# Sketched attention and a gated convolution on one core: tokens of a chunk in the order (m, j), stores by group

## The chip, the cores and the metric

The kernel runs on one core of a Trainium2 chip. The metric is the device time of one execution in microseconds (us), the median over the runs of the unchanged kernel.

## What is computed

The inputs are q, k and v of shape 4 x 4 x 1088 x 32 (batch, heads, tokens, head dimension), two sketch matrices S1 and S2 of 8 x 32, and three weights. Attention is linear: both q and k become 64 features, products of two sketches of 8. Its output, heads side by side, is x of 4 x 1088 x 128; xp is x with K - 1 = 4 rows of zeros ahead of each batch, so the gate is a causal convolution of 5 taps for each channel.

```python
def phi(x):
    a = np.einsum('rd,bhsd->bhsr', S1, x)
    b = np.einsum('rd,bhsd->bhsr', S2, x)
    return np.einsum('bhsi,bhsj->bhsij', a, b).reshape(*x.shape[:-1], r * r)
q_p, k_p = (phi(q), phi(k))
kv = np.einsum('bhsf,bhsd->bhfd', k_p, v)
z = np.sum(k_p, axis=2)
num = np.einsum('bhsf,bhfd->bhsd', q_p, kv)
den = np.einsum('bhsf,bhf->bhs', q_p, z)[..., None] + 1e-06
return (num / den).astype(np.float32)
...
x = np.ascontiguousarray(attn_out.transpose(0, 2, 1, 3)).reshape(B, S, H * D)
...
for k in range(K):
    gate_pre += conv_w[k][None, None, :] * xp[:, k:k + S, :]
gate = 1.0 / (1.0 + np.exp(-gate_pre))
val = x @ w_val
return (gate * val @ w_out).astype(np.float32)
```

## The kernel before

The 1088 tokens of a batch are seen as 32 values of m times 34 values of t, token = 34 m + t, so that one m is a contiguous piece of 34 tokens in memory. The t are cut into two units, U = 0 with t from 16 to 33 and U = 1 with t from 0 to 15, and into four groups of 8 or 10 t (`GROUPS`). The last two t (32 and 33) are the leftover, `v_lo` and `osb_lo`. For products with tokens on the partitions a chunk of 128 tokens is 4 values of j times 32 values of m, with t = 8 j + c for k and v and t = t0 + 4 j + c at the output.

All work is cut into steps with names of four characters: two letters for the kind, a digit for the batch (0 to 3) and a digit for a unit, group or part. The table `ORDER` lists all steps, and the loop at the end of the kernel issues them in that order, so it sets the order of instructions on each engine; numbers behind a colon are the PSUM banks (`ring`) that a step uses. Nothing is rescheduled. Each engine works off its own instructions in order.

The kinds are, in the order in which a batch passes through them: `ld` loads (0 and 1 the weights, from ACT's queue; 2 and 3 the halves of k with t below 16 and from 16 on, 4 and 5 those of q from 16 on and below 16, 6 v in four transfers, one for a head, 7 the leftover of v in two; all from SP's queue). `kt` transposes k on DVE, `kp` multiplies it with the sketches on PE, `ke` copies the result to SBUF on ACT (`kab`), `ko` forms the 64 features (`phik`) on POOL or DVE, `kv` sums them against v and z on PE. `pv`, `pz`, `pm`, `pe` turn these sums into weights (`wq`, `kvb`). `qt`, `qp`, `qc`, `qd`, `qo` do the same for q, with the denominator (`phi`), `qx` transposes on PE, `qe` copies (`phiT`), `nm` multiplies with kv, `xe` copies to `xe`, and `hl` shifts the first columns. `gt` is the convolution and `vl` the value product on PE, `sg` the sigmoid on ACT, `gv` their product on DVE, `om` the output product on PE, `oe` its copy to `osb` on ACT, and `so` the stores from SP's queue. `cn` are constants, `cn06` nine matmuls on zeros ahead of the real ones, `cn05` the casts of two weights on POOL. The sets `KO_DVE` and `QO_POOL` say which products go to DVE and which to POOL.

Every load has a buffer of its own, for each batch, so no load waits for compute.

Of the kernel before, what the change touches and what calls it, by code (L numbers as in the profile page):

```python
# [24 lines left out]


ORDER = """
cn08 ld00 cn00 ld02 cn06:01 ld03 cn07 ld06 cn09 ld01 ld07 cn02
cn01 ld05 kt00 ld04 ld13 ld12 kt01 ld15 kp00:2 ld16 kp01:3 ke00
ko00 ko03 ke01 ko02 ko08 ko09 ld23 cn03:4 ko06 cn04 cn05 ld17  # L30
ko05 ko01 ko07 kv00 qt01 ld14 ld22 kv01 ld26 qt00 pv00 pz00
pm00:5 kt11 pe00 ld25 qp00:6 kt10 ld32 ld33 qp01:0 qc00 ld35 qt11
kp10:1 ld24 qc01 qd00 kp11:3 ld27 ke10 ko12 ke11 ld36 ko13 qd01
ko11 qo01 ko16 ld37 ko10 qo00 qx01:2 ko18 kv10 qo02 qe01 ld34
ko17 qx00:4 qt10 qx02:5 ko15 nm01:1 qe00 qo03 qe02 ko19 nm00:3 kt21
qx03:6 xe01 nm02:2 kv11 xe00 hl00 kt20 qe03 xe02 nm03:4 pz10 pv10
kp20:0 xe03 pm10:5 qt21 ke20 kp21:1 pe10 ko20 ko21 gt01:36 ke21 ko23
kt30 vl03:2 vl02:4 sg03 ko25 ko27 qp10:5 sg02 gv03 ko22 gv02 qp11:0
qc10 kt31 ko29 om01:6 kv20 qc11 qd10 ko28 oe01 kp30:1 ko26 so01
kp31:3 qt20 ke30 qo10 kv21 qo11 gt00:24 ko31 pv20 ko32 ke31 pz20  # L40
ko33 vl01:6 qd11 sg00 pm20:5 sg01 ko39 qx11:1 pe20 vl00:2 qx10:4 qe11
ko30 gv01 qp20:5 qe10 qo13 ko36 nm11:1 kv30 qc20 qo12 ko37 xe11
nm10:6 gv00 ko38 qx13:4 ko35 qx12:1 xe10 om00:02 qd20 qe13 hl10 kv31
qe12 oe00 nm13:3 nm12:6 pz30 qp21:4 qo21 qo20 pv30 so00 xe12 xe13
pm30:1 qt30 qc21 qx20:0 gt11:26 pe30 qd21 qe20 vl12:5 vl13:3 sg13 nm20:1
qx21:0 sg12 gv13 qp30:6 xe20 qo23 gv12 qe21 qt31 om11:4 gt10:23 qc30
qo22 oe11 qd30 vl10:1 so11 vl11:5 sg10 nm21:0 sg11 qx23:4 qp31:2 xe21
gv11 qe23 hl20 qx22:3 gv10 qc31 nm23:0 qo31 qe22 qo30 om10:54 xe23
nm22:1 qd31 oe10 qx30:3 gt20:60 xe22 so10 qe30 vl20:4 vl21:5 qo33 qo32
qx31:1 sg20 nm30:3 sg21 gv20 qx33:6 qe31 gt21:20 gv21 qe33 vl23:4 vl22:1  # L50
xe30 nm31:5 nm33:6 sg23 qx32:3 xe31 gv23 qe32 om20:05 hl30 xe33 nm32:4
oe20 gt30:36 xe32 so20 vl30:0 sg22 vl31:5 sg30 gt31:42 gv22 sg31 gv30
om21:3 gv31 sg33 vl32:1 vl33:6 sg32 om30:02 oe21 gv33 gv32 oe30 so21
om31:5 so30 oe31 so31
""".split()


# [1 line left out]
def kernel(  # L59
# [94 lines left out]
    def s_const(b, i):  # L154
        if i == 0:
            nc.gpsimd.memset(mask1, 1.0)
            for sgn, base in ((1, 0), (-1, 31)):
# [10 lines left out]
        elif i == 9:
            make_identity(nc, ident32)
            make_identity(nc, ident)  # L170
            for t in range(2):
                nc.gpsimd.memset(pden[t], 1e-6)
                nc.gpsimd.memset(xe[t][:, 0:4, 0:1], 0.0)
                nc.gpsimd.memset(kvb[t], 0.0)
        elif i == 1:
            nc.vector.transpose(sT[:, 0, :], s1raw)
            nc.vector.transpose(sT[:, 1, :], s2raw)
            for t in range(2):
                nc.vector.tensor_mul(
                    wq[t][:, 0:64].rearrange("p (k h r) -> p k h r", k=2, h=H),  # L180
                    bc(sT[:, :, 0:r], 2, [P, 2, H, r]),
                    bc(bc(mask1, 1, [P, 2, 4]), 3, [P, 2, 4, r]),
                )
        elif i == 2:
            nc.vector.tensor_reduce(
                out=mask2, in_=mask16.rearrange("p c h -> p h c"), axis=AX.X, op=ALU.add
            )
            nc.vector.tensor_mul(
                s2rep.rearrange("p (h d) -> p h d", h=H),
                bc(s2raw, 1, [P, H, D]),  # L190
                bc(mask2, 2, [P, H, D]),
            )
        elif i == 3:
            nc.tensor.transpose(bank("cn", b, i)[:, 0:Kconv], cw_in, ident32[:Kconv, :Kconv])
        elif i == 4:
            nc.scalar.copy(out=cwT, in_=bank("cn", 0, 3)[:, 0:Kconv])
# [4 lines left out]
        elif i == 5:
            nc.gpsimd.tensor_copy(out=wv, in_=wv_f)
            nc.gpsimd.tensor_copy(out=wo, in_=wo_f)
# [8 lines left out]
    def s_ld(b, i):
# [9 lines left out]
        elif i in (2, 3, 4, 5):  # L222
            x, y = ((k, k_in), (q, q_in))[i // 4]
            t0, n = ((0, 16), (16, 18), (16, 18), (0, 16))[i - 2]
            nc.sync.dma_start(  # L225
                out=y[b][:, t0 * D : (t0 + n) * D],
                in_=x[b].rearrange("h (m t) d -> (h m) (t d)", m=M)[:, t0 * D : (t0 + n) * D],
            )
        elif i == 6:
            for h in range(H):  # L230
                nc.sync.dma_start(  # L231
                    out=v_in[b][:, h, :],
                    in_=v[b, h].rearrange("(m t) d -> m (t d)", m=M)[:, 0:1024].rearrange("m (j x) -> j m x", j=4),
                )
        elif i == 7:
            for j in range(2):
                nc.sync.dma_start(
                    out=v_lo[b][j * 32 : j * 32 + 32],
                    in_=v[b].rearrange("h (m t) d -> m h t d", m=M)[:, :, 32 + j, :],
                )  # L240

    def s_kt(b, u):
        o = kT[b % 2][:, 0:32, :].rearrange("p (c j) m -> p j c m", j=4)[:, 2 * u : 2 * u + 2]
        i_ = k_in[b][:, 0 : 32 * D].rearrange("p (j c d) -> p j c d", j=4, c=8)[:, 2 * u : 2 * u + 2]
        nc.vector.transpose(o, i_)  # L245
# [14 lines left out]
    def s_ke(b, u):  # L260
        nc.scalar.copy(out=kab[u][:, :, 0 : 4 + u, :], in_=kab_view(b, u))  # L261
# [153 lines left out]
    def s_gv(b, g):  # L415
# [4 lines left out]
        nc.vector.tensor_mul(  # L420
            o[:, 0:512].rearrange("p (c j m) -> p j c m", c=4, j=4)[:, 2 * w : 2 * w + 2], view(gate[g]), view(vl)
        )
        if g == 1:
            nc.vector.tensor_mul(o[:, 512:576], gate[g][:, 256:320], vl[:, 256:320])

    def s_om(b, U):
# [10 lines left out]
        if U == 0:  # L437
            nc.scalar.copy(out=osb_lo[b], in_=bank("om", b, U, 1)[0:64, 0:P])

    def s_so(b, U):  # L440
        t0, n = UNITS[U]
        dst = out[b].rearrange("(m t) e -> m t e", m=M)
        nc.sync.dma_start(
            out=dst[:, t0 : t0 + 16, :].rearrange("m (j c) e -> j m (c e)", j=4),
            in_=osb[2 * b + U].rearrange("p c e -> p (c e)"),
        )
        if U == 0:
            nc.sync.dma_start(out=dst[:, 32:34, :].rearrange("m j e -> j m e"), in_=osb_lo[b])
# [39 lines left out]
```

## Time and profile before

| | us |
|---|---|
| median of 3 runs | 75.9 (75.12 to 76.77) |
| the profiled execution | 74.68 |
| its span, from the first to the last instruction | 72.8 |

Busy time over the span is 48.5 on PE, 38.6 on DVE, 35.1 on ACT and 27.2 on POOL. The span is the part that the trace shows; 1.88 us of the profiled execution lie around it. In the rows of the prediction a stretch of the span, 35.00:59.83 for instance, is followed by its length and by the busy time of each engine in it with the number of instructions in brackets. A line such as L245 is a line of the listing above. A row of waits names who waited, for whom, the total in us, how many times and the longest. SPq is SP's sequencer, which issues the transfers, and its durations are those of an issue, not of a transfer.

### The profile page before, as it was taken

How to read it: one execution, taken by the hardware profiler on the slowest of the kernel's cores; microseconds unless marked ns; L12 is line 12 of the kernel's file. 1: busy time of each engine (PE TensorE's matmuls, PEld its weight loads, DVE VectorE, ACT ScalarE, POOL GpSimd, SP SyncE). 2: the span in 40 equal slices, each digit the busy share in tenths (PEclk: the TensorE clock that was granted, in tenths of full speed). 3: DMA queues.
4: the chain of work that ended last, by engine and by line, in shares of the span. 5: the costliest groups of instructions: out<-in, count | busy, mean ns of one | idle time of the engine just before them, and what ended most of it. 6: DMA issues, size and time to landing. Idle time of an engine off the chain costs nothing.

```text
span 72.8 us, 2687 instructions
## 1 busy us (share of the span) xinstructions
PE 48.5 (67%) x1114; PEld 37.3 (51%) x1114; DVE 38.6 (53%) x103; ACT 35.1 (48%) x100; POOL 27.2 (37%) x58
## 2 busy tenths in 40 slices
PE   3962949689537599946999999999998950000000
PEld 1312927479426379824978887877786630000000
DVE  1029477666991931079998979969852540000000
ACT  0800490121523746722449799989999891000000
POOL 5900345000499500991199816655731000000000
PEclk9999655555999857999999999999999999655555
DMA  0935469838753499532563201222222222222220
GB/s 0 285 118 155 128 217 279 300 105 222 242 166 108 139 304 297 170 111 91 131 197 106 101 35 18 62 81 36 82 74 88 62 52 96 48 99 101 98 94 11
DMA packets 7645, 9.30 MB, mean 128 GB/s; under 512 B 1869, under 2 KB 4562, under 8 KB 7634
## 3 DMA queue, kind: packets, MB, share of 16 engines
q1 hardware_dynamic: 6888, 8.91, 39.5%
q10 hardware_dynamic: 746, 0.23, 1.5%
q8 instruction: 8, 0.13, 0.7%
q14 instruction: 3, 0.02, 0.1%
HBM read 6.92 MB, written 2.23 MB: 126 GB/s over the span
## 4 chain that ended last, share of the span: by engine, by line
DMA 32%; PE 27%; SPq 9%; ACT 7%; DVE 4%; issue 3%; DVEq 0%; ACTq 0%
PE ring L138 18%; DMA k_in<-in_k_dram 12%; DMA q_in<-in_q_dram 11%; DMA v_in<-in_v_dram 9%; SPq L231 6%; PE kv L138 5%; PE ring L375 4%; SPq L225 3%; ACT phiT L381 2%; ACT gate L409 2%; ACT osb L436 2%; DVE gv L420 1%; DVE kT L245 1%; DVE qT L323 1%; PE ring L309 1%
## 5 line engine op out<-in xcount | busy, mean ns | idle before, releaser
L268 POOL TENSOR_TENSOR phik<-kab 128x256 f32<-128x256 f32 x26 | 15.4, 626 | 15.8 <-ACT kab L261 15.5
L381 ACT COPY phiT<-ring 128x512 bf16<-128x512 bf16 (+1 forms) x16 | 9.4, 617 | 3.6 <-PE ring L375 2.9
L361 POOL TENSOR_TENSOR phi<-an,bc_sb 128x512 bf16<-128x512 f32 (+1 forms) x6 | 7.3, 1217 | 6.9 <-DVE an L353 3.5
L138 PE MATMUL ring<-wq,qT 128*64 128x96 f32 x144 | 8.7, 278 | 1.4 <-DVE phik L268 1.1
L323 DVE STREAM_TRANSPOSE qT<-q_in 128x512 f32<-128x512 f32 (+1 forms) x8 | 5.9, 742 | 6.2 <-DMA q_in<-in_q_dram 6.1
L138 PE MATMUL kv<-phik,v_in 128*32 128x64 f32 x256 | 7.8, 256 | 1.9 <-DMA v_in<-in_v_dram 1.1
L138 PEld LDWEIGHTS ring<-wq,qT 128*64 128x64 f32 x144 | 7.6, 159 | 1.9 <-DVE phik L268 1.3
L375 PE MATMUL ring<-ident,phi 128*64 128x128 bf16 (+1 forms) x144 | 7.0, 224 | 2.2 <-DVE phi L361 2.2
L420 DVE TENSOR_TENSOR gv<-gate,ring 128x256 bf16<-128x256 bf16 x16 | 6.2, 415 | 3.3 <-ACT gate L409 3.2
L138 PE MATMUL ring<-wq,kT 128*64 128x64 f32 x144 | 6.3, 242 | 1.9 <-DVE kT L245 1.9
L138 PEld LDWEIGHTS kv<-phik,v_in 128*32 128x32 f32 x256 | 5.8, 129 | 3.3 <-DMA v_in<-in_v_dram 1.3
L361 DVE TENSOR_TENSOR phi<-an,ring 128x512 bf16<-128x512 f32 (+1 forms) x10 | 7.0, 728 | 0.3 <-POOL phik L268 0.2
L375 PEld LDWEIGHTS <-phi 128*64 128x64 bf16 (+1 forms) x144 | 5.4, 112 | 3.4 <-DVE phi L361 2.5
L138 PEld LDWEIGHTS ring<-wq,kT 128*64 128x64 f32 x144 | 5.8, 155 | 2.7 <-DVE kT L245 2.5
L138 PE MATMUL ring<-xe,diag 64*64 64x256 bf16 (+1 forms) x160 | 6.5, 280 | 0.0
L261 ACT COPY kab<-ring 128x256 f32<-128x256 f32 (+1 forms) x8 | 3.2, 399 | 6.6 <-PE ring L138 6.1
L391 ACT CAST xe<-ring 128x256 bf16<-128x256 f32 (+1 forms) x16 | 6.2, 400 | 0.4 <-PE ring L138 0.4
L409 ACT ACTIVATE gate<-ring 128x256 bf16<-128x256 f32 (+1 forms) x16 | 5.6, 405 | 0.5 <-PE ring L138 0.5
L245 DVE STREAM_TRANSPOSE kT<-k_in 128x512 f32<-128x512 f32 x8 | 5.5, 692 | 0.6 <-DMA k_in<-in_k_dram 0.6
L342 ACT COPY bc_sb<-ring 128x320 f32<-128x320 f32 (+3 forms) x8 | 2.8, 355 | 5.2 <-PE ring L138 5.1
L138 PE MATMUL ring<-phiT,kvb 128*64 128x256 bf16 (+1 forms) x32 | 4.7, 306 | 0.7 <-ACT phiT L381 0.6
L436 ACT COPY osb<-ring 128x512 f32<-128x512 f32 x8 | 4.7, 602 | 0.9 <-PE ring L138 0.8
(56 smaller groups left out, 66.1 us busy)
## 6 DMA issues: line engine op xcount, KB each, us to landing
v_in<-in_v_dram SPq DMA_DIRECT2D x16, 128.0 KB
out_dram<-osb SPq DMA_DIRECT2D x8, 256.0 KB
k_in<-in_k_dram SPq DMA_DIRECT2D x4, 288.0 KB
q_in<-in_q_dram SPq DMA_DIRECT2D x4, 288.0 KB
k_in<-in_k_dram SPq DMA_DIRECT2D x4, 256.0 KB
q_in<-in_q_dram SPq DMA_DIRECT2D x4, 256.0 KB
v_lo<-in_v_dram SPq DMA_DIRECT2D x8, 16.0 KB
out_dram<-osb_lo SPq DMA_DIRECT2D x4, 32.0 KB
```

Of the source, the lines that this page charges most:

```text
L138: nc.tensor.matmul(o, lhsT=lhsT, rhs=rhs, start=start, stop=stop, skip_group_check=True, **kw)
L231: nc.sync.dma_start(out=v_in[b][:, h, :], in_=v[b, h].rearrange("(m t) d -> m (t d)", m=M)[:, 0:1024].rearrange("m (j x) -> j m x", j=4),)
L245: nc.vector.transpose(o, i_)
L268: (nc.vector if dve else nc.gpsimd).tensor_mul(phik[u][:, c].rearrange("p h (i j) -> p h i j", i=r), bc(a_, 3, [P, H, r, r]), bc(b_, 2, [P ...
L323: nc.vector.transpose(flat(qT[b % 2][:, t0 : t0 + n, :]), q_in[b][:, t0 * D : (t0 + n) * D])
L361: (nc.gpsimd if pool else nc.vector).tensor_mul(phi[(4 * b + g) % 3][:, 0:n, :].rearrange("p c (i j) -> p c i j", i=r), bc(an[U][:, lo : l ...
L375: nc.tensor.transpose(o[64 * (h % 2) : 64 * (h % 2) + 64, h // 2, c * P : c * P + n], phi[(4 * b + g) % 3][:n, 4 * c + h, :], ident[:n, :n],)
L381: nc.scalar.copy(out=phiT[(4 * b + g) % 3][:, :, 0 : GROUPS[g][1] * M], in_=pt_view(b, g))
L391: nc.scalar.copy(out=flat(xe[b % 2][:, 4 + t0 : 4 + t0 + n, :]), in_=bank("nm", b, g)[:, 0 : n * M])
L409: nc.scalar.activation(out=gate[g][:, 0:n], in_=bank("gt", b, g // 2, g % 2)[:, 0:n], func=ACT.Sigmoid)
L420: nc.vector.tensor_mul(o[:, 0:512].rearrange("p (c j m) -> p j c m", c=4, j=4)[:, 2 * w : 2 * w + 2], view(gate[g]), view(vl))
L436: nc.scalar.copy(out=osb[2 * b + U].rearrange("p c e -> p (c e)"), in_=bank("om", b, U))
```

## The change

A chunk of 128 tokens now has its tokens in the order (m, j) instead of (j, m). So the transfers of v and the stores have m, with 32 values, as outermost dimension where they had j, with 4 or 2. Four things follow from it: the transposed k (`kT`) is written with j as the innermost dimension, so neighbours are 4 elements apart; `gv` is written in the same way, 2 elements apart; a chunk's two halves of 64 partitions belong to one group each, so each group is stored by itself (two stores of 64 partitions for a unit in place of one of 128); and the matmul of `kp` takes 64 adjoining columns. Apart from that, the second `wq` is copied from the first, the tables `KO_DVE` and `QO_POOL` are other, with one phi product less on POOL, and `ORDER` is a new table.

```diff
-cn08 ld00 cn00 ld02 cn06:01 ld03 cn07 ld06 cn09 ld01 ld07 cn02
+cn08 ld00 cn09 ld04 cn06:01 ld03 cn07 ld02 ld05 ld07 cn00 ld01
...
-    kT = [st(f"kT{i}", [P, NT, M]) for i in range(2)]
+    kT = [st(f"kT{i}", [P, NT * M]) for i in range(2)]
...
-            for t in range(2):
-                nc.vector.tensor_mul(
-                    wq[t][:, 0:64].rearrange("p (k h r) -> p k h r", k=2, h=H),
...
+            nc.vector.tensor_mul(
+                wq[0][:, 0:64].rearrange("p (k h r) -> p k h r", k=2, h=H),
...
         elif i == 2:
+            nc.vector.tensor_copy(out=wq[1][:, 0:64], in_=wq[0][:, 0:64])
...
-                    in_=v[b, h].rearrange("(m t) d -> m (t d)", m=M)[:, 0:1024].rearrange("m (j x) -> j m x", j=4),
+                    in_=v[b, h].rearrange("(m t) d -> m (t d)", m=M)[:, 0:1024].rearrange("m (j x) -> m j x", j=4),
...
-        o = kT[b % 2][:, 0:32, :].rearrange("p (c j) m -> p j c m", j=4)[:, 2 * u : 2 * u + 2]
+        o = kT[b % 2][:, 0:1024].rearrange("p (c m j) -> p j c m", c=8, m=M)[:, 2 * u : 2 * u + 2]
...
-            t = 16 * u + 4 * c
-            two = [t, t + 2] if c < 4 else [32, 32]
+            t = 512 * u + P * c
             for z in range(2):
-                mm(o[64 * z : 64 * z + 64, :, c, :], flat(kT[b % 2][:, two[z] : two[z] + 2, :]), wq[0][:, 0:64])
+                lt = kT[b % 2][:, t + 64 * z : t + 64 * z + 64] if c < 4 else kT[b % 2][:, 1024:1088]
+                mm(o[64 * z : 64 * z + 64, :, c, :], lt, wq[0][:, 0:64])
...
-            o[:, 0:512].rearrange("p (c j m) -> p j c m", c=4, j=4)[:, 2 * w : 2 * w + 2], view(gate[g]), view(vl)
+            o[:, 0:512].rearrange("p (c w m j) -> p w j c m", c=4, w=2, m=M)[:, w], view(gate[g]), view(vl)
...
-    def s_so(b, U):
-        t0, n = UNITS[U]
+    def s_so(b, g):
+        t0, n = GROUPS[g]
+        w = g % 2
         dst = out[b].rearrange("(m t) e -> m t e", m=M)
         nc.sync.dma_start(
-            out=dst[:, t0 : t0 + 16, :].rearrange("m (j c) e -> j m (c e)", j=4),
-            in_=osb[2 * b + U].rearrange("p c e -> p (c e)"),
-        )
-        if U == 0:
-            nc.sync.dma_start(out=dst[:, 32:34, :].rearrange("m j e -> j m e"), in_=osb_lo[b])
...
+            out=dst[:, t0 : t0 + 8, :].rearrange("m (j c) e -> m j (c e)", j=2),
+            in_=osb[2 * b + g // 2][64 * w : 64 * w + 64].rearrange("p c e -> p (c e)"),
+        )
+        if g == 1:
+            nc.sync.dma_start(out=dst[:, 32:34, :], in_=osb_lo[b])
```

Below, a number behind a name is that of a buffer: q_in_75 to q_in_78, k_in_71 to k_in_74, v_in_79 to v_in_82 and v_lo_83 to v_lo_86 belong to batches 0 to 3, osb_125 to osb_132 to unit 0 and 1 of batches 0 to 3 in turn, phik_93 and kab_91 to the chunks with u = 0 and phik_94 and kab_92 to those with u = 1.

The start of SP's queue, the loads of batch 0 and the first of batch 1:

```order
+L225 DMA q_in_75<-in_q_dram 128x576
+L225 DMA k_in_71<-in_k_dram 128x576
 L225 DMA k_in_71<-in_k_dram 128x512
-L225 DMA k_in_71<-in_k_dram 128x576
+L225 DMA q_in_75<-in_q_dram 128x512
+L237 DMA v_lo_83<-in_v_dram 32x4x32 x2
 L231 DMA v_in_79<-in_v_dram 128x1x256 x4
-L237 DMA v_lo_83<-in_v_dram 32x4x32 x2
-L225 DMA q_in_75<-in_q_dram 128x512
-L225 DMA q_in_75<-in_q_dram 128x576
+L225 DMA k_in_72<-in_k_dram 128x512
 L225 DMA k_in_72<-in_k_dram 128x576
```

Both halves of q now stand ahead of v, and one of them ahead of k. Up to q of batch 2 (the last part of q_in_77) the new queue has q and k of three batches, v of two, and the leftovers of three, 26 transfers; v of batch 2, which stood ahead of it, stands behind k of batch 3.

PE between the weights of batch 0 (`pm00`) and the first transposes of phi, before:

```order
L138 MATMUL ring_69<-zm_95,s2rep 64x32 x2
L309 MATMUL ring_69<-ident_139,kvf_97 128x128
L138 MATMUL ring_70<-wq_101,qT_89 64x3x32 x10
L138 MATMUL ring_64<-wq_101,qT_89 64x3x32 x8
L138 MATMUL ring_65<-wq_101,kT_88 64x2x32 x8
L138 MATMUL ring_67<-wq_101,kT_88 64x2x32 x10
```

and now:

```order
L138 MATMUL ring_69<-zm_95,s2rep 64x32 x2
L309 MATMUL ring_69<-ident_139,kvf_97 128x128
L138 MATMUL ring_70<-wq_101,kT_88 64x2x32 x8
L138 MATMUL ring_64<-wq_101,qT_89 64x3x32 x10
L138 MATMUL ring_65<-wq_101,kT_88 64x2x32 x10
L138 MATMUL ring_66<-wq_101,qT_89 64x3x32 x8
```

The two halves of `kp` of batch 1 (kT_88) moved ahead of one half of `qp` of batch 0 (qT_89) each. On POOL the two weight casts (`cn05`) moved from behind the first two products of batch 0 to ahead of them, and of batch 1's nine products `ko` two went to DVE.

The end of SP's queue, the stores of batch 2 and 3, before:

```order
L443 DMA out_dram<-osb_129 4x32x512
L448 DMA out_dram<-osb_lo_135 2x32x128
L443 DMA out_dram<-osb_130 4x32x512
L443 DMA out_dram<-osb_131 4x32x512
L448 DMA out_dram<-osb_lo_136 2x32x128
L443 DMA out_dram<-osb_132 4x32x512
```

and now:

```order
L445 DMA out_dram<-osb_130 32x2x512 x2
L445 DMA out_dram<-osb_129 32x2x512 x2
L450 DMA out_dram<-osb_lo_135 32x2x128
L445 DMA out_dram<-osb_131 32x2x512 x2
L450 DMA out_dram<-osb_lo_136 32x2x128
L445 DMA out_dram<-osb_132 32x2x512 x2
```

Each store of 4 x 32 pieces became two of 32 x 2, and behind the copy of the last unit (osb_132) two stores follow in place of one.

More of the change, by code (lines that the diff above doesn't have):

```diff
@@ L36 @@
[L36 to L51, printed above, removed]
@@ L55 @@
+qo33 qe30 vl23:5 so10 qo32 vl22:1 sg23 qx33:3 nm30:0 sg22 nm31:2 gv23
+xe30 qx32:6 gv22 xe31 gt20:45 qe33 hl30 qe32 om21:0 nm33:2 sg20 vl20:1
+vl21:3 nm32:6 xe33 gv20 sg21 gt30:42 xe32 gv21 oe21 vl31:1 sg31 om20:56
+so23 vl30:3 sg30 gt31:02 gv31 so22 oe20 gv30 vl32:4 vl33:1 sg33 so20
+om30:56 sg32 gv33 so21 oe30 gv32 om31:3 so30 oe31 so31 so32 so33
 """.split()
@@ L246, in s_kt @@
         if u == 1:
-            nc.vector.transpose(flat(kT[b % 2][:, 32:34, :]), k_in[b][:, 32 * D : 34 * D])
+            nc.vector.transpose(kT[b % 2][:, 1024:1088], k_in[b][:, 32 * D : 34 * D])
     def kab_view(b, u):
```

42 lines of the change are left out of this document (27 added, 15 removed).

## The prediction

> **What bounds the kernel now.** I read the page's slices first, then the chain that ended last, then the busy time by stretches that I cut where the slices change.
>
> ```profile
> span 72.8 us, 2687 instructions
> PE   3962949689537599946999999999998950000000
> PEclk9999655555999857999999999999999999655555
> DMA  0935469838753499532563201222222222222220
> HBM read 6.92 MB, written 2.23 MB: 126 GB/s over the span
> DMA 32%; PE 27%; SPq 9%; ACT 7%; DVE 4%; issue 3%; DVEq 0%; ACTq 0%
> ...
> 3.67 6.73 DMA v_in<-in_v_dram
> ...
> 14.07 8.55 DMA k_in<-in_k_dram
> ...
> 23.22 8.13 DMA q_in<-in_q_dram
> ...
> 59.86 0.58 ACT osb L436
> ```
>
> There are three parts. Until 31.35 (23.22 + 8.13) the chain is made of loads and their issue. Then compute runs to 60.44 (59.86 + 0.58), with PE at nine tenths. Then come 12.4 us (72.8 - 60.44) with all engines still and only the DMA row at 2 tenths.
>
> ```profile
> 6.48:20.00 13.52, 10.45 (x204) 8.79 (x204) 9.21 (x24) 4.55 (x16) 3.32 (x7) 0.62 0.69 210
> 20.00:35.00 15.00, 10.66 (x283) 8.39 (x283) 8.36 (x19) 6.83 (x19) 8.86 (x16) 0.89 0.55 172
> 35.00:59.83 24.83, 23.78 (x626) 18.91 (x618) 18.99 (x54) 21.64 (x63) 12.21 (x16) 1.00 0.28 80
> 64.00:71.00 7.00, 0.00 (x0) 0.00 (x0) 0.00 (x0) 0.00 (x0) 0.00 (x0) 0.50 0.26 98
> 71.00:72.80 1.80, 0.00 (x0) 0.00 (x0) 0.00 (x0) 0.00 (x0) 0.00 (x0) 0.50 0.03 11
> ...
> 25.00:30.00 5.00, 5.00 (x123) 4.08 (x121) 1.34 (x4) 2.55 (x9) 1.02 (x3) 0.68 0.97 283
> ...
> SPq L483 <- DMA out_dram<-osb: 9.2, 1, 9.2
> ...
> SPq L237 <- DMA v_in<-in_v_dram: 5.0, 3, 2.3
> ...
> POOL phik L268 <- ACT kab L261: 15.5, 3, 7.0
> DVE qT L323 <- DMA q_in<-in_q_dram: 6.1, 3, 3.8
> ```
>
> Columns are the stretch and its length, then PE, PEld, DVE, ACT and POOL busy time, granted clock, DMA share, GB/s. In 64 to 71 only stores are left: share 0.26 and 98 GB/s, about 4 of 16 engines at 25 GB/s each. With all engines busy (25 to 30) the same hardware moves 283 GB/s at 0.97. Every transfer whose outermost dimension is 4 (v_in, osb) is confined to a quarter of the engines, and whatever is spread over all of them (k_in, q_in) waits for that quarter. That is why POOL, DVE and PE starve before 35.
>
> **The change, part by part.**
>
> *1. The tail.* The rows at the end:
>
> ```profile
> 59.85 0.54 SPq L443 DMA_DIRECT2D out_dram<-osb  x1
> 60.48 0.62 SPq L448 DMA_DIRECT2D out_dram<-osb_lo  x1
> 61.20 1.29 SPq L443 DMA_DIRECT2D out_dram<-osb  x1
> ...
> L443 SPq DMA_DIRECT2D out_dram<-osb x8: 537/548/1288, 35.4 to 61.2; - x8
> ...
> L231 SPq DMA_DIRECT2D v_in<-in_v_dram x16: 531/532/755, 1.7 to 32.7; - x16
> ...
> 59.53 0.28 ACT L438 COPY osb_lo<-ring 64x128 f32<-64x128 f32 x1
> ...
> 0.80 0.88 SPq L225 DMA_DIRECT2D k_in<-in_k_dram  x2
> ...
> 1.50:2.00 0.50, 0.50 (x2) 0.15 (x1) 0.00 (x0) 0.00 (x0) 0.38 (x3) 1.00 0.36 66
> ```
>
> After, the last stores are two for unit 0, one small, two for unit 1. At 0.55 each (median 0.548) five take 2.75, and four gaps of 0.09 (59.85 + 0.54 to 60.48) make 3.1. They begin when the copy of unit 0 is done, about 0.9 before that of unit 1 ends (0.58 for it and 0.28 for osb_lo between), so SP is through 2.2 after the last copy. Before it was 2.05 (61.20 + 1.29 - 60.44), so the doubled issues cost next to nothing: the long last issue, which waited for the queue, pays for them. Then the first byte: the first load, issued at 0.80 for 0.44, shows 33 KB in the stretch 1.5 to 2.0, so bytes from about 1.88, 0.65 after its issue. The last 131 KB at 283 GB/s take 0.47. From the last bytes (20 KB move after 71.0, so to about 71.1) to the end of the span are 1.7. Sum: 2.2 + 0.65 + 0.47 + 1.7 = 5.0 instead of 12.4, a gain of 7.4. Ends: 4.4 if one issue less is left behind the copy, 6 if the last two stores follow one another at half the rate.
>
> [...]
>
> *2. Loads.* The 2.1 MB of v now use all engines, so the whole stream goes at 283 GB/s. What DVE waited for until 31.37, q of batch 2, has 4.5 MB of k, q and v up to its own end in the new SP order (front part), plus 0.2 MB of weights: 4.7 / 0.283 = 16.6, from 1.9 on, plus 1.7 to its semaphore as at the span's end: 20. k of batch 3, 0.56 MB more, lands by about 22. SP's issue is not in the way: 26 transfers up to there at 0.53, the median of v's (k and q take less), are 13.8. From 20 on no engine should wait for loads. What is late next is compute.
>
> *3. The first 20 us.* Here latency, not bandwidth, sets the pace.
>
> ```profile
> 4.90 0.29 DVE L188 TENSOR_TENSOR s2rep<-s2raw,mask 128x128 f32<-128x128 f32 x1 [2.64 <-DMA s2raw<-in_S_dram]
> ...
> 5.72 1.29 DVE L245 STREAM_TRANSPOSE kT<-k_in 128x512 f32<-128x512 f32 x2
> ...
> 6.48 0.33 PE L138 MATMUL ring<-wq,kT 128*64 128x64 f32 x2 [1.60 <-DVE kT L245]
> ...
> 15.01 3.14 PE L138 MATMUL ring<-wq,qT 128*64 128x96 f32 x36 [0.28 <-ACT wq L313]
> 17.94 1.25 PE L138 MATMUL ring<-wq,kT 128*64 128x64 f32 x36
> ...
> 11.12 0.40 POOL L203 CAST wo<-wo_f 128x256 bf16<-128x256 f32 x1 [1.01 <-DMA wo_f<-in_moe_w_out_dram]
> ...
> 19.15 5.29 POOL L268 TENSOR_TENSOR phik<-kab 128x256 f32<-128x256 f32 x9 [7.05 <-ACT kab L261]
> ...
> L323 DVE STREAM_TRANSPOSE qT<-q_in 128x512 f32<-128x512 f32 x4 | 2.8, 710 | 4.6 <-DMA q_in<-in_q_dram 4.5
> ```
>
> One q transpose (at least 0.71, as the smaller half has it) and the constants now stand ahead of the first kT on DVE, so the first kp starts about 1.0 later, near 7.5. The v wait that follows (v landed at 10.4) goes, since v of batch 0 is 1.7 MB into the stream (landing near 9.5). Both casts stand ahead of all products on POOL, and the cast of wo waited until 11.12 for its load. POOL's products take 0.59 (5.29 / 9). Of batch 0's three only the last stood behind that cast: 11.5 + 0.6 = 12.1. If the load comes no earlier, the three now end near 13.3; if it lands at 10, near 12.2. I take the first qp at 15.3, and PE at 20.0 where it was. What is gained is order: the first half of kp of batch 1 now runs ahead of qp, POOL has seven products of batch 1 instead of nine (two went to DVE, which idles there), and the last five start behind the second half of kp, near 18.2: 18.2 + 5 x 0.59 = 21.1, three us sooner than 24.4 (19.15 + 5.29). kv of batch 1 follows them.
>
> *4. From 20 on.* PE's rate when nothing starves it is 23.78 / 626 = 0.038 per matmul. The 283 + 626 = 909 left at 20.0 need 34.5, so PE could end at 54.5 and ended at 59.83: 4.3 were lost before 35 (15.0 - 283 x 0.038) and 1.05 after. Of the 4.3 I give back 3.0: loads and POOL, which caused the waits, come early, but the chain phi, phiT, nm, xe of batch 0 leaves PE thin near 20, and a stretch at clock 0.5 may come again (the mean in 20 to 35 is 0.89). Ends: 0 and 4.3. ACT needs 6.83 + 21.64 = 28.5 after 20 and DVE 27.4, both below PE.
>
> *5. Strides.*
>
> ```profile
> L245 DVE STREAM_TRANSPOSE kT<-k_in 128x512 f32<-128x512 f32 x8 | 5.5, 692 | 0.6 <-DMA k_in<-in_k_dram 0.6
> L420 DVE TENSOR_TENSOR gv<-gate,ring 128x256 bf16<-128x256 bf16 x16 | 6.2, 415 | 3.3 <-ACT gate L409 3.2
> ```
>
> kT is now written with 16 bytes between neighbours, gv with 4. kT already is scattered by blocks and costs 692 against 710 for the plain qT of the same size, so I take 0; the other end is twice the time, 5.5 + 6.2 = 11.7 on DVE. A gain is left out, as qT, written in one piece, is no faster. One phi product goes from POOL to DVE and one product for wq becomes a copy, less than 1 us of DVE together; its idle time (15.0 - 8.36 before 35) hides that, and under the second rival it would not.
>
> **Sum.** Compute ends at 60.44 - 3.0 = 57.4; with 5.0 the span is 62.4 instead of 72.8, minus 10.4. The profiled execution took 74.68 (1.88 outside its span), 1.2 below the median 75.9: 64.3 by the one, 65.5 by the other. I say 64.9, midway, that is 2.5 above the span, here and for the rivals.
>
> **Rivals.**
> - *Only the tail goes.* ACT is busy 21.64 of 24.83 in the dense stage and the later start of kp is real; then compute ends at 60.4 and the time is 60.4 + 5.0 + 2.5 = 67.9.
> - *The strides cost.* With 11.7 more, DVE needs 36.4 after 20 (27.4, half of kT's 5.5 and all of gv's 6.2), more than PE's 34.5: with 2 to 3 of waits compute ends near 59, and the time is 66.5. Against it speaks the kT row above. [...]
> - *PE runs dense from 20 on.* The 4.3 go whole, and the last 1.05 too: compute ends at 55.1, the time is 62.6.
> - *It does not do what it says.* If 4 engines stay, the tail and the loads stay: 75 to 76. The 0.97 with k_in and q_in (outermost 128) speaks against it.
> - *Slower.* If the split follows the dimension that counts j wherever it stands, it is 2 for the stores now. Then 2.23 MB go at 2 x 25 = 50 GB/s, 44.6 us. In the new order no output matmul stands ahead of kv of batch 3, and some 16 us of PE work stand behind the first, so the first store comes near 40: span 86, time 89. It turns into a loss when the stores get less than about 65 GB/s (2.23 MB in 33 us). The rows can't tell the place of the 4 from its being 4.
>
> [...]
>
> **How the numbers follow.** Both gains 0.60, tail alone 0.18, strides 0.08, dense 0.08, no effect 0.03, slower 0.03. Changes over 2% are about what a measurement of this kernel can tell from none. Faster by over 2% holds the first four, 0.94; within 2% 0.03; slower 0.03. The range reaches from the dense case with a tail of 4.4 (61.5) to the tail alone with a tail of 6 (69).
>
> **What would show it.** Right: after the last osb copy under 6 us, a DMA share above 0.5 while stores run, no DVE wait of over 1 us for q_in, the last PE instruction between 55 and 58.5, kT still near 0.69. Wrong: share 0.26 or 0.13 at the end; kT near 1.4; PE at clock 0.5 beyond 22; PE gaps between 20 and 30 released by ACT or DVE rather than DMA, which would make the order the bound.

## The result, and the profile after

| | before | changed |
|---|---|---|
| median, us | 76.34 (75.12 to 77.3, 4 runs) | 65.1 (64.98 to 65.72, 4 runs) |
| the profiled execution | 74.68 | 64.98 |
| its span | 72.8 | 63.0 |
| the last copy to osb ends | 60.44 | 56.80 |
| from there to the end of the span | 12.4 | 6.2 |

The ratio is 0.864, with a 95% interval of 0.852 to 0.876. The forecast was 64.9. Of the 9.8 us that the span lost, 6.2 went from the tail and 3.6 from compute. Some executions are disturbed and a little longer; ratios leave them out, and medians here are over all runs of a kernel.

The page of the changed kernel, its slices (a slice is now 1.575 us) and its chain:

```profile
span 63.0 us, 2682 instructions
PE   2990019388799959997999999999979998920000
DVE  1015991991935999999999999995898916730000
ACT  0630002650421407788248999599999999970000
PEclk9999855555555899999999999999999999999655
DMA  0799469988669993773400000019136530386650
PE 30%; DVE 27%; ACT 22%; DMA 6%; issue 2%; ACTq 1%; DVEq 1%
```

The chain was a third DMA; now it is compute, and of the DMA share only one load is left, that of S2 at the very start. DMA is busy until slice 20 and then only while stores run, where before it dragged on at 1 and 2 tenths from slice 25 to the end. The 2 tenths of the tail have become 5 and 6, and the tail is short.

Busy time by stretches of the changed kernel (columns as in the prediction):

```profile
6.48:20.00 13.52, 9.13 (x180) 8.02 (x182) 9.02 (x19) 3.87 (x14) 3.73 (x7) 0.53 0.79 241
20.00:35.00 15.00, 13.80 (x431) 11.41 (x427) 14.57 (x35) 8.73 (x25) 11.30 (x19) 0.96 0.52 160
...
20.00:30.00 10.00, 8.80 (x241) 7.13 (x237) 9.78 (x21) 5.91 (x17) 6.44 (x12) 0.95 0.71 213
30.00:40.00 10.00, 10.00 (x355) 8.54 (x357) 9.62 (x26) 7.02 (x22) 7.95 (x13) 1.00 0.09 30
40.00:56.80 16.80, 14.82 (x341) 11.30 (x339) 11.82 (x34) 16.25 (x46) 4.75 (x6) 1.00 0.42 97
```

Up to 20 PE is behind where it was (180 matmuls, before 204). Then it is far ahead: 431 against 283 in 20 to 35. The bound wanders: DVE is full from 20 to 30 (9.78 of 10), PE from 30 to 40 (10.00), ACT from 40 to the end (16.25 of 16.80). No engine waits for k_in, q_in or v_in any more.

The start, rows of the timeline on DVE, PE and POOL:

```profile
5.31 0.21 DVE L177 STREAM_TRANSPOSE sT<-s2raw 128x32 f32<-128x32 f32 x1 [0.66 <-DMA s2raw<-in_S_dram]
...
6.42 0.77 DVE L323 STREAM_TRANSPOSE qT<-q_in 128x576 f32<-128x576 f32 x1
7.11 1.04 DVE L245 STREAM_TRANSPOSE kT<-k_in 128x512 f32<-128x512 f32 x1
...
8.12 1.02 DVE L245 STREAM_TRANSPOSE kT<-k_in 128x512 f32<-128x512 f32 x1
...
9.20 2.19 PE L138 MATMUL ring<-wq,kT 128*64 128x64 f32 x36 [4.49 <-DVE kT L245]
...
17.83 1.81 PE L138 MATMUL ring<-wq,qT 128*64 128x96 f32 x20
...
7.86 0.40 POOL L203 CAST wo<-wo_f 128x256 bf16<-128x256 f32 x1 [0.77 <-DMA wo_f<-in_moe_w_out_dram]
...
21.32 2.97 POOL L268 TENSOR_TENSOR phik<-kab 128x256 f32<-128x256 f32 x5 [1.51 <-ACT kab L261]
```

and the groups of the two tiles that are written at a stride (group rows of the page):

```profile
L245 DVE STREAM_TRANSPOSE kT<-k_in 128x512 f32<-128x512 f32 x8 | 8.5, 1090 | 0.0
...
L420 DVE TENSOR_TENSOR gv<-gate,ring 128x256 bf16<-128x256 bf16 x16 | 6.6, 439 | 2.8 <-ACT gate L409 2.4
```

The k transpose takes 1090 ns where it took 692. The first kp waits for two of them and starts at 9.20, where it was 6.48 before and 7.5 in the forecast. Before, two matmuls of kp could start when one half of kT was written, and the other 34 stood at 7.07:

```profile
7.07 1.63 PE L138 MATMUL ring<-wq,kT 128*64 128x64 f32 x34 [0.26 <-DVE kT L245]
```

Now 64 adjoining columns hold all four values of j, so even the first matmul needs both halves. The cast of wo, on the other hand, is over at 8.26, long before POOL's first product needs the engine.

The end, rows of the timeline on ACT and SP and stretches of the tail:

```profile
56.21 0.59 ACT L437 COPY osb<-ring 128x512 f32<-128x512 f32 x1 [0.33 <-PE ring L138]
...
53.32 2.46 SPq L445 DMA_DIRECT2D out_dram<-osb  x4
55.87 0.55 SPq L450 DMA_DIRECT2D out_dram<-osb_lo  x1
56.51 1.19 SPq L445 DMA_DIRECT2D out_dram<-osb  x2
57.79 0.55 SPq L450 DMA_DIRECT2D out_dram<-osb_lo  x1
58.44 1.19 SPq L445 DMA_DIRECT2D out_dram<-osb  x2
...
59.63:60.20 0.57, 0.00 (x0) 0.00 (x0) 0.00 (x0) 0.00 (x0) 0.00 (x0) 0.50 0.93 212
60.20:60.70 0.50, 0.00 (x0) 0.00 (x0) 0.00 (x0) 0.00 (x0) 0.00 (x0) 0.50 0.88 205
60.70:61.20 0.50, 0.00 (x0) 0.00 (x0) 0.00 (x0) 0.00 (x0) 0.00 (x0) 0.50 0.34 78
```

From 53.32 on SP issues without a pause, ten stores in 6.3 us, so the last one is issued 2.8 behind the last copy (59.63). From there on some 260 KB move, both of the last stores (0.57 x 212 + 0.50 x 205 + 0.50 x 78), at 205 to 212 GB/s with the engines at 0.9.

### The profile page after: what moved, and what is told of

It reads as the page before. It is cut to its first block, busy times and chain, and to the rows that moved or that the text cites. A ratio compares the mean times of both kernels' runs of the same rounds, so it can differ in the third digit from the quotient of the medians.

```text
span 63.0 us, 2682 instructions
## 1 busy us (share of the span) xinstructions
PE 46.2 (73%) x1114; PEld 36.1 (57%) x1114; DVE 41.7 (66%) x104; ACT 34.5 (55%) x100; POOL 25.6 (41%) x57
## 4 chain that ended last, share of the span: by engine, by line
PE 30%; DVE 27%; ACT 22%; DMA 6%; issue 2%; ACTq 1%; DVEq 1%
PE ring L138 19%; DVE kT L245 11%; PE kv L138 9%; ACT phiT L381 7%; DMA s2raw<-in_S_dram 6%; ACT gate L409 5%; ACT osb L437 5%; DVE phi L361 4%; ACT xe L391 3%; PE ring L375 2%; DVE phik L268 2%; DVE qT L323 2%; DVE den L351 2%; DVE pden L350 1%; ACT bc_sb L342 1%
## 5 line engine op out<-in xcount | busy, mean ns | idle before, releaser
L138 PE MATMUL ring<-wq,kT 128*64 128x64 f32 x144 | 7.2, 271 | 5.1 <-DVE kT L245 4.5
L261 ACT COPY kab<-ring 128x320 f32<-128x320 f32 (+1 forms) x8 | 3.2, 399 | 10.4 <-PE ring L138 9.6
L245 DVE STREAM_TRANSPOSE kT<-k_in 128x512 f32<-128x512 f32 x8 | 8.5, 1090 | 0.0
L361 DVE TENSOR_TENSOR phi<-an,ring 128x512 bf16<-128x512 f32 (+1 forms) x11 | 7.9, 748 | 0.1
L361 POOL TENSOR_TENSOR phi<-an,bc_sb 128x512 bf16<-128x512 f32 (+1 forms) x5 | 5.7, 1158 | 4.4 <-DVE zm L297 2.6
L138 PE MATMUL kv<-phik,v_in 128*32 128x64 f32 x256 | 6.6, 245 | 1.2 <-POOL phik L268 1.0
L138 PEld LDWEIGHTS kv<-phik,v_in 128*32 128x32 f32 x256 | 5.0, 124 | 2.2 <-POOL phik L268 1.2
L323 DVE STREAM_TRANSPOSE qT<-q_in 128x576 f32<-128x576 f32 (+1 forms) x8 | 5.8, 724 | 0.0
L268 DVE TENSOR_TENSOR phik<-ring,kab 128x256 f32<-128x256 f32 x10 | 3.7, 414 | 2.4 <-ACT kab L261 2.4
L138 PEld LDWEIGHTS <-diag 64*64 64x64 bf16 x160 | 4.4, 106 | 1.3 <-issue 0.8
```

The costliest lines, as they stand in the source:

```text
L138: nc.tensor.matmul(o, lhsT=lhsT, rhs=rhs, start=start, stop=stop, skip_group_check=True, **kw)
L268: (nc.vector if dve else nc.gpsimd).tensor_mul(phik[u][:, c].rearrange("p h (i j) -> p h i j", i=r), bc(a_, 3, [P, H, r, r]), bc(b_, 2, [P ...
L323: nc.vector.transpose(flat(qT[b % 2][:, t0 : t0 + n, :]), q_in[b][:, t0 * D : (t0 + n) * D])
L361: (nc.gpsimd if pool else nc.vector).tensor_mul(phi[(4 * b + g) % 3][:, 0:n, :].rearrange("p c (i j) -> p c i j", i=r), bc(an[U][:, lo : l ...
```

## Experiments

Twelve kernels were measured in three groups of four; those of a group ran on the same chip. "First kp" is the start of the first matmuls of kp on PE, "compute ends" the end of the last copy to osb, both from the profiled execution.

### The loads alone, the stores alone, both, under the old order table

Both the loads of v and the stores can have 32 outermost values without a new token order, if a transfer takes one j instead of one head or one unit: then m is outermost, and the tokens stay in the order (j, m). For v this needs as many transfers as before, for the stores four times as many. Three kernels do one, the other, and both, with everything else as in the kernel before.

```diff
-            for h in range(H):
+            for j in range(4):
                 nc.sync.dma_start(
-                    out=v_in[b][:, h, :],
-                    in_=v[b, h].rearrange("(m t) d -> m (t d)", m=M)[:, 0:1024].rearrange("m (j x) -> j m x", j=4),
+                    out=v_in[b][32 * j : 32 * j + 32, :, :],
+                    in_=v[b].rearrange("h (m t) d -> m h (t d)", m=M)[:, :, 256 * j : 256 * j + 256],
                 )
...
-        nc.sync.dma_start(
-            out=dst[:, t0 : t0 + 16, :].rearrange("m (j c) e -> j m (c e)", j=4),
-            in_=osb[2 * b + U].rearrange("p c e -> p (c e)"),
-        )
+        for j in range(4):
+            nc.sync.dma_start(
+                out=dst[:, t0 + 4 * j : t0 + 4 * j + 4, :].rearrange("m c e -> m (c e)"),
+                in_=osb[2 * b + U][32 * j : 32 * j + 32].rearrange("p c e -> p (c e)"),
+            )
         if U == 0:
-            nc.sync.dma_start(out=dst[:, 32:34, :].rearrange("m j e -> j m e"), in_=osb_lo[b])
+            for j in range(2):
+                nc.sync.dma_start(out=dst[:, 32 + j, :], in_=osb_lo[b][32 * j : 32 * j + 32])
```

Loads alone:

> The kernel before, only v's loads cut by j instead of by head, so that m with 32 values is their outermost dimension; token order, stores and order table as before. Theory of the prediction (confined loads starve compute until 35): the last copy to osb ends near 57 instead of 60.4, no wait of DVE for q_in over 1 us, but the tail stays at 11 to 12.5, since the stores stay on 4 engines: 71.5 to 73. Rival (the new order table is what makes compute end earlier): compute ends at 60 still, 75 to 76.

Stores alone:

> The kernel before, only the stores cut by j, four of 32 partitions for a unit with m as outermost dimension, and two for the leftover; loads and order table as before. Theory: compute ends at 60.4 as before, and the tail is bound by SP's issue, some 10 stores at 0.6 behind the copy of unit 0 and then 3.4 to the end: 8.9 behind the last copy instead of 12.4, so 71 to 73. Rival (tail bound by the engines' rate, whatever the issues): 5 to 6, so 68 to 69.

Both:

> Both at once, with the order table of before. Theory: the gains add, compute ends near 57 and the tail is 8.9: 67.5 to 69.5. Rival (the order table is needed for the gain of compute): 71 to 73, as with the stores alone.

| | median, us | ratio to before (95%) |
|---|---|---|
| loads alone | 72.97 (71.98 to 73.85) | 0.940 (0.929 to 0.950) |
| stores alone | 71.77 (70.64 to 73.56) | 0.926 (0.909 to 0.943) |
| both | 68.21 (67.44 to 69.05) | 0.888 (0.875 to 0.901) |

All three times lie where the theory had them, and none where a rival had it. By ratios the gains are 6.0% and 7.4%, together 11.2%, so most of the sum is kept. The loads end compute earlier and the stores shorten the tail. With the loads alone (a profile of 73.85) the last copy ends at 58.54, not quite the 57 expected, and the tail is 13.4; DVE's waits for q_in, 6.1 before, are gone. With the stores alone (a profile of 71.91) it ends at 62.37 and the tail is 7.8, and those waits are there still:

```profile
DVE qT L323 <- DMA q_in<-in_q_dram: 5.7, 3, 3.9
```

The kernel with both has both gains in its profile (PE's first kp, ACT's last copy, SP's last issues):

```profile
6.80 0.33 PE L138 MATMUL ring<-wq,kT 128*64 128x64 f32 x2 [1.59 <-DVE kT L245]
...
56.37 0.59 ACT L436 COPY osb<-ring 128x512 f32<-128x512 f32 x1
...
55.79 4.94 SPq L444 DMA_DIRECT2D out_dram<-osb  x8
60.83 0.84 SPq L450 DMA_DIRECT2D out_dram<-osb_lo  x2
61.77 1.77 SPq L444 DMA_DIRECT2D out_dram<-osb  x4
```

Compute ends at 56.96, as in the changed kernel (56.80), without its order table and without its strides. What it lacks is the tail: 65.7 - 56.96 = 8.7, since fourteen issues stand in SP's queue from 55.79 to 63.54. The changed kernel needs half as many stores and has 6.2.

### The order table

The changed kernel under the table and the sets `KO_DVE` and `QO_POOL` of before, with `so` by group in the place of `so` by unit.

```diff
-cn08 ld00 cn09 ld04 cn06:01 ld03 cn07 ld02 ld05 ld07 cn00 ld01
+cn08 ld00 cn00 ld02 cn06:01 ld03 cn07 ld06 cn09 ld01 ld07 cn01
...
-    KO_DVE = {(0, 1), (0, 2), (0, 3), (0, 6), (0, 7), (0, 9), (1, 1), (1, 3), (2, 1), (3, 2)}
+    KO_DVE = {(0, 0), (0, 1), (0, 2), (0, 5), (0, 6), (0, 9), (2, 1), (2, 5), (3, 2), (3, 5)}
```

> The changed kernel with the order table and the two sets of before (stores by group in the place of those by unit, two constants exchanged since the copied wq needs it). Theory (the new table itself brings nothing to the end of compute, as with loads and stores alone under the old table it ended at 57.0): compute ends at 56.5 to 57.8, tail 6.2, 65 to 66.5. Rival (the new table is worth 2 us or more): 67 to 69.

The changed kernel itself ran beside it and beside the next two, as the measure:

> The changed kernel itself, as the measure for the three that run beside it: 64.8 to 65.7, last copy to osb near 56.8, tail 6.2.

It took 65.91 (65.69 to 66.45, 6 runs), 0.8 more than at first; its compute ended at 57.64 and its tail was 6.3. Under the old table it took 66.86 (65.72 to 67.82), a little above the 65 to 66.5 that was expected, and in its profile (of 66.89) compute ended at 58.67. The median is 0.95 higher, but the two lowest runs of each are equal (65.72 and 65.97 against 65.69 and 65.72). So no worth of the new table is shown, and one of 2 us or more is out.

### How many engines a store uses

The output side back in the order (j, m), one store for a group as in the changed kernel, so the outermost dimension of a store is j with 2 values. k, v and the table are as changed.

```diff
-            out=dst[:, t0 : t0 + 8, :].rearrange("m (j c) e -> m j (c e)", j=2),
+            out=dst[:, t0 : t0 + 8, :].rearrange("m (j c) e -> j m (c e)", j=2),
             in_=osb[2 * b + g // 2][64 * w : 64 * w + 64].rearrange("p c e -> p (c e)"),
...
-            nc.sync.dma_start(out=dst[:, 32:34, :], in_=osb_lo[b])
+            nc.sync.dma_start(out=dst[:, 32:34, :].rearrange("m j e -> j m e"), in_=osb_lo[b])
```

> The changed kernel with the output side back in the order (j, m), so that a store by group has j, with 2 values, as outermost dimension; k, v and the order table as changed. Theory (the outermost dimension sets how many engines a transfer uses): a DMA share of 0.13 and about 50 GB/s while only stores run, the stores of 2.2 MB take 44 from the first at 41, so 85 to 90, slower than the kernel before. Rival (they use 4 engines as the stores of before did, or are spread anyway): share 0.26 or more, 65 to 72.

It took 93.73 (92.83 to 94.32), 1.232 times the kernel before (1.221 to 1.244). A stretch of its tail:

```profile
62.00:85.00 23.00, 0.00 (x0) 0.00 (x0) 0.00 (x0) 0.00 (x0) 0.00 (x0) 0.50 0.13 50
```

A share of 0.13 is 2 of 16 engines, and 50 GB/s is half of the 98 of the kernel before. With outermost 4, 2 and 32 the shares of stores alone are 0.26 (before, 64 to 71), 0.13 (here) and 0.88 to 0.93 (changed, 59.63 to 60.70), so in these three the share goes with the outermost dimension. The time missed the expected 85 to 90 by 4: the first store was issued at 42, only 28 GB/s moved on average from 35 to 55, and at 50 GB/s (48 from 85 to 90) the rest lasted until about 90. So the fall from 4 engines to 2 that the prediction named as a rival is real when j is the outermost dimension; the change averts it by putting m there.

### The tail

Four of the last stores go to other queues: the leftovers of batches 2 and 3 and group 1 of batch 3 to POOL's, group 3 of batch 3 to ACT's.

```diff
         w = g % 2
+        eng = {(3, 1): nc.gpsimd, (3, 3): nc.scalar}.get((b, g), nc.sync)
...
-        nc.sync.dma_start(
+        eng.dma_start(
             out=dst[:, t0 : t0 + 8, :].rearrange("m (j c) e -> m j (c e)", j=2),
...
-            nc.sync.dma_start(out=dst[:, 32:34, :], in_=osb_lo[b])
+            (nc.gpsimd if b >= 2 else nc.sync).dma_start(out=dst[:, 32:34, :], in_=osb_lo[b])
```

> The changed kernel, with four of the last stores on other queues: the leftovers of batches 2 and 3 and group 1 of batch 3 from POOL's, group 3 of batch 3 from ACT's, the rest from SP's as before. Theory (the tail is 6.2 instead of 5.0 because ten issues stand in one queue at 0.6 each from 53.3 on): SP is through near 57.5, the tail is 4.0 to 4.6, the time 63.0 to 63.7. Rival (the tail is bound by stores of 64 partitions, which move at about 205 GB/s): no more than 0.5 is gained, 64.6 to 65.2.

It took 63.57 (63.08 to 64.08), 2.3 less than the changed kernel beside it, as the theory had it. Its last issues on SP and ACT, and a stretch of its tail (the last copy ended at 57.67):

```profile
50.15 8.09 SPq L446 DMA_DIRECT2D out_dram<-osb  x7
...
57.70 0.63 ACTq L446 DMA_DIRECT2D out_dram<-osb  x1
...
57.67:60.00 2.33, 0.00 (x0) 0.00 (x0) 0.00 (x0) 0.01 (x1) 0.30 (x1) 0.82 0.85 246
```

All are issued by 58.33, 0.7 behind the last copy instead of 2.8, and the tail is 62.0 - 57.67 = 4.3. So 2 of the 6.3 in the changed kernel beside it were SP's issue. The rest is the transfer and the wait for its end.

### The start

The first q transpose of batch 0 moved behind the two k transposes, in the table alone.

```diff
-ld06 cn01 cn02 qt00 ld12 ld13 kt01 ld14 ld16 kt00 kp01:2 qt01
+ld06 cn01 cn02 ld12 ld13 kt01 ld14 ld16 kt00 kp01:2 qt00 qt01
```

> The changed kernel, with the first q transpose of batch 0 behind the two k transposes instead of ahead of them on DVE, nothing else. Theory (the first kp starts at 9.2 because of what stands ahead of it on DVE, and the start carries through): first kp 0.7 earlier, compute ends 0.5 to 0.9 earlier, 64.2 to 64.6. Rival (from 30 on PE and then ACT set the end whatever the start): 65.0 to 65.3.

It took 64.93 (64.39 to 65.79), above the 64.2 to 64.6 of the theory and just below the rival's 65.0; but the changed kernel beside it took 65.91 and not 65.1, so the gain is 1.0, clear of the rival. First kp and last copy of the changed kernel beside it, then of this one:

```profile
9.89 1.34 PE L138 MATMUL ring<-wq,kT 128*64 128x64 f32 x20 [4.61 <-DVE kT L245]
...
57.06 0.58 ACT L437 COPY osb<-ring 128x512 f32<-128x512 f32 x1 [0.33 <-PE ring L138]
```

```profile
9.37 1.87 PE L138 MATMUL ring<-wq,kT 128*64 128x64 f32 x30 [4.09 <-DVE kT L245]
...
56.45 0.58 ACT L437 COPY osb<-ring 128x512 f32<-128x512 f32 x1 [0.33 <-PE ring L138]
```

The start moved by 0.52 and the end by 0.61, so the start carries through, and the rival, by which later bounds swallow it, falls. One pair of profiles could do this by chance, but all agree: in the six of kernels with the new table and the stride, the first kp starts at 9.20 to 10.32, and from there to the end of the last copy it is 47.6 to 47.8 in each.

### The stride

The changed kernel, with k and v alone back in the order (j, m). v's loads are cut by j as in the first experiment, which keeps m outermost and the number of transfers, and kT is written without gaps. The output side stays in the order (m, j).

```diff
-        o = kT[b % 2][:, 0:1024].rearrange("p (c m j) -> p j c m", c=8, m=M)[:, 2 * u : 2 * u + 2]
+        o = kT[b % 2][:, 0:32, :].rearrange("p (c j) m -> p j c m", j=4)[:, 2 * u : 2 * u + 2]
```

> The changed kernel, with k and v alone back in the token order (j, m), v's loads cut by j so that m is still outermost; kT is written without gaps; output side, stores and order table as changed. Theory (the 16-byte stride costs DVE 0.4 for each kT): kT back at 0.69, the first kp at 8.5 instead of 9.2, DVE 3.2 less busy, compute ends 0.7 to 2 earlier: 63.1 to 64.4. Rival (DVE has room, so the stride costs nothing of the time): 65.0 to 65.2. Second rival (the stride is not what slows kT): kT stays at 1.09 and the time too.

It took 64.67 (64.2 to 65.61), above the 63.1 to 64.4 of the theory and below the 65.0 of the rival; the changed kernel's 65.1 is of another group. Against the kernel before, measured beside each, the ratios are 0.840 (0.831 to 0.849) and 0.864 (0.852 to 0.876), which would be 1.8 us. kT was back at 0.684, so the stride is what slows it. But S2 landed 0.8 later in its profile (its transpose began at 6.08), the first kp started at 9.44, and compute ended at 56.64, hardly sooner. By itself this left the price in the time open. So the two edits that helped were put together, once with the stride and once without, side by side:

> The changed kernel with the two edits that helped, k ahead of q at the start of DVE and the last stores on three queues; kT still written at a stride of 16 bytes. Theory (they act at the two ends and add): 1.0 + 2.3 less than the 65.9 of the changed kernel beside them, 62.3 to 63.0. Rival (they overlap): 63.4 to 63.8.

> The same, with k and v in the token order (j, m) and v's loads cut by j, so that kT is written without gaps. Theory (the stride costs 0.4 for each kT, two of them ahead of all work, and DVE is full from 20 to 30): compute ends 0.8 to 1.5 sooner than in the run with the stride beside it, and the time is as much less. Rival (later limits, PE from 30 and ACT from 40 on, swallow it): within 0.3 of that run.

With the stride it took 63.06 (62.75 to 63.37), 0.835 of before (0.830 to 0.841), just above the 62.3 to 63.0 that was expected. Without the stride it took 61.26 (60.95 to 62.26), 0.810 (0.805 to 0.815). Their profiles, with the stride (the transposes, in ns least, median and most; the stretch in which DVE is full; the last copy):

```profile
L245 DVE STREAM_TRANSPOSE kT<-k_in x8: 1028/1093/1139, 7.1 to 28.9; 128x512 f32<-128x512 f32 x8
...
20.00:30.00 10.00, 9.04 (x241) 7.37 (x237) 9.70 (x21) 5.89 (x18) 6.37 (x12) 0.92 0.84 245
...
56.28 0.59 ACT L437 COPY osb<-ring 128x512 f32<-128x512 f32 x1 [0.34 <-PE ring L138]
```

and without:

```profile
L245 DVE STREAM_TRANSPOSE kT<-k_in x8: 669/698/705, 7.3 to 27.0; 128x512 f32<-128x512 f32 x8
...
20.00:30.00 10.00, 8.75 (x295) 7.51 (x291) 9.76 (x25) 6.13 (x19) 7.77 (x14) 1.00 0.86 225
...
54.30 0.59 ACT L437 COPY osb<-ring 128x512 f32<-128x512 f32 x1 [0.33 <-PE ring L138]
```

The first kp starts 0.5 sooner (8.75 and 9.27) and compute ends 2.0 sooner. DVE is as full in 20 to 30, but it gets through 25 instructions instead of 21, and PE starts 295 matmuls instead of 241. The stride costs 1.8 us of the time in this pair, more than the expected 0.8 to 1.5. That DVE is the bound in the middle fits this, as eight transposes at 0.4 less are 3.2 of its time. The pair differs also in how v's loads are cut, but no engine waits for v_in in the profile of the changed kernel, nor in that of the kernel above, which cuts them by j. How much is lost behind the start is less sure: from the first kp to the end of the last copy it is 47.6 to 47.8 with the stride, and 47.2, 46.1 and 46.8 in the three profiles without it (the kernel above, this one, and the next). The kernel without the stride is the fastest of the study, by 0.810 against 0.864 of the change.

### The load of S2

Of the fastest kernel, the load of S1 moved from ACT's queue to the front of SP's, so that S2 is first on ACT's.

```diff
-            nc.scalar.dma_start(out=s1raw, in_=bc(S1, 0, [16, r, D]))
+            nc.sync.dma_start(out=s1raw, in_=bc(S1, 0, [16, r, D]))
```

> The same as the one without gaps, with the load of S1 as the first on SP's queue, ahead of q and k, so that S2 is the first on ACT's. Theory (the chain begins with the small load of S2, which is issued second and lands at 5.3 to 6.2): S2 lands 0.7 or more sooner, the first kp starts 0.5 to 1.2 sooner and the end follows by 0.4 to 1.2. Rival (k, now issued 0.6 later, lands last): the first kp moves by less than 0.2, or later.

It took 61.8 (61.37 to 62.32), 0.820 of before (0.813 to 0.827), no gain over the 61.26 beside it. Its start:

```profile
3.49 0.17 DVE L177 STREAM_TRANSPOSE sT<-s2raw 128x32 f32<-128x32 f32 x1
...
6.26 0.71 DVE L245 STREAM_TRANSPOSE kT<-k_in 128x512 f32<-128x512 f32 x1 [1.62 <-DMA k_in<-in_k_dram]
...
7.72 0.71 DVE L245 STREAM_TRANSPOSE kT<-k_in 128x512 f32<-128x512 f32 x1 [0.62 <-DMA k_in<-in_k_dram]
...
8.49 2.19 PE L138 MATMUL ring<-wq,kT 128*64 128x64 f32 x36 [3.21 <-DVE kT L245]
```

S2 was there 2.7 sooner (the transpose began at 3.49 instead of 6.16), but then k was late, by 1.62 and 0.62, and the first kp gained 0.26. Compute ended at 55.24 instead of 54.89. The first half of the theory holds and the second fails: the wait moved from S2 to k. Loading k ahead of q as well was not tried.

## Why the prediction was right, point by point

- **The cause** (a quarter of the engines carries v and the stores) holds: the share was 0.26 in the tail of before. Loads and stores changed alone gain 6.0% and 7.4%, both 11.2%, and stores with 2 outermost values make the kernel 1.23 times as long.
- **The tail, 5.0, was 6.2.** Two terms were too small. SP was through 2.8 behind the last copy and not 2.2: I let the last five issues begin when the copy of unit 0 was done, but SP still had the stores of batch 2 to issue (it starts those of batch 3 at 56.51, though the copy ended at 55.73). The end, 2.8 by 0.65 + 0.47 + 1.7, took 3.4: both of the last stores moved after the last issue, 262 KB instead of 131, at 205 to 212 GB/s and not at 283. This is near the end that the prediction named as 6. The 283 came from a row of 128-partition loads, and these stores have 64 partitions; that this is the reason is not shown, and the stores spread over three queues moved 246.
- **The loads** no longer hold up any engine, as forecast. They were not as fast as forecast, and "SP's issue is not in the way" was wrong: the first 26 transfers, put at 13.8, took until 18.04, 17.2 after the first. The 26th is the second of this row, q of batch 2:

```profile
17.13 0.91 SPq L225 DMA_DIRECT2D q_in<-in_q_dram  x2
```

The loads of k of batch 3 were issued from 18.32 on, and loads of k took a median of 3.8 to 4.1 us to land, so this k came, by estimate, later than 22; but its transpose stood at 27.8 on DVE anyway. The last load was issued at 26.9.
- **The first 20 us.** "PE at 20.0 where it was" was wrong: the first qp came at 17.83 instead of 15.3. The first kp was 1.7 later than the 7.5 forecast: 0.6 because it now needs both halves of kT (7.07 against 6.48 before), which the prediction overlooked, 0.8 by the two strided transposes and 0.4 by S2, which together make it up. POOL's five products for batch 1 ended at 24.29, not 21.1, so their gain of three us went into the late start. The new order, from which this gain was to come, shows no worth in its own experiment. The feared wait for wo did not come.
- **From 20 on.** "PE's rate when nothing starves it", 0.038 for a matmul, is not a rate of PE but a mean over kinds that cost differently, as these two rows of before show for 35 to 59.83:

```profile
L138 PE MATMUL ring<-xe,diag 64*64 64x256 bf16 x100 | 5.2, 273 | 0.0
L138 PE MATMUL kv<-phik,v_in 128*32 128x64 f32 x104 | 2.6, 222 | 0.0
```

The one kind takes 0.052 of PE's busy time for each matmul, the other 0.025. In 30 to 40 of the changed kernel 128 of 355 are of the cheaper kind, before 104 of 626, and the mean there is 0.028. PE had 937 matmuls left at 20 and not 909, since the start was later, but they took 33.6 of busy time, 0.036 each, and not 34.5. The idle time that was left was forecast well: 2.5 up to PE's last matmul at 56.2, against 1.3 + 1.05 = 2.35. Compute ended at 56.8 instead of 57.4.
- **The sum.** Its three terms missed by -0.6 (compute, 56.8 for 57.4), +1.2 (the tail, 6.2 for 5.0) and -0.4 (what lies outside the span, 2.1 for 2.5), and met within 0.2. That the time came so near is luck; the causes and the rough shares of tail and compute are not. The low end of the range is also off by its own terms: 55.1 + 4.4 + 2.5 is 62.0 and not 61.5.
- **The strides.** "I take 0" for kT was wrong: 692 became 1090, 0.4 each. I judged by a row whose neighbours are contiguous, within a block, and took it for a scattered one; the run without the stride confirms the size (a median of 698, beside 1093 with it). At 4 bytes gv went from 415 to 439, nearly nothing. Why 16 bytes cost and 4 hardly do is not shown. The rival that the strides cost had a chance of 0.08 and was half true: they cost, 1.8 us by the pair that ran side by side, and the time still came out as forecast.
- **The signs.** Of those for right, the absence of long waits for q_in and the last PE instruction (56.2) came; the tail missed its 6 by 0.2, and kT left 0.69. The DMA share was above 0.5 in most of the stretches with stores alone, not in all (0.34 from 60.70 to 61.20). One sign of wrong came too: PE's longest gaps between 20 and 30, 0.65 and 0.36, were released by DVE. There the order of work on DVE has become the bound.

## What to carry to other kernels

Give a transfer a larger outermost dimension, 32 here (a share of about 0.9 for stores alone) in place of 4 or 2 (0.26 and 0.13), before anything is rearranged for it: cutting it along the small dimension did that here for v without a new layout. The layout that was made for transfers was paid for by DVE, which wrote it (1.09 us for 0.69 a transpose), so look at the stride in bytes at which each engine then writes, and at whether its reader now has to wait for more of it, as the first kp did here. And a mean time per instruction belongs to the mix that it was taken from: count the kinds before carrying it to another stretch.

## What the runs showed of the hardware

- The transposes of k on DVE, 128x512 f32, took 1.09 us with neighbours written 16 bytes apart, in the changed kernel and in the one with both edits, and 0.68 to 0.70 with neighbours adjoining, in the kernel before and in the three without the stride.
- Stores with 2, 4 and 32 outermost values kept 0.13, 0.26 and about 0.9 of the 16 engines busy and moved 50, 98 and 205 to 212 GB/s, each in a stretch with stores alone (the last in stores of 64 partitions); with the last ones issued from three queues it was 246 GB/s from 57.67 to 60.00.
- One 16 KB load landed late: that of S2, issued second on ACT's queue at 1.5, was waited for until 5.0 to 6.4 in the profiles of the changed kernel and its variants, and it was there by 3.5 when it was issued first.
- The granted clock hardly mattered. The changed kernel took 64.98 and 65.11 with a mean granted clock of 0.857 and 0.866, and 65.1 and 65.72 with 0.98 and 0.974. In the profile the low clock, 0.5, stands in the slices from 7.9 to 20.5 us, while PE is busy for 9.13 of the 13.52 from 6.48 to 20; that this is why it costs nothing is not shown.
